# Linear attention and a two-layer squared-ReLU product: Strassen products over pairs of blocks

## The chip, the cores and the metric

The kernel runs on one core of a Trainium2 chip. The metric is the device time of one execution in microseconds (us); of several executions the median counts. Busy times, waits and the order in time come from one profiled execution.

## What is computed

```python
k_s = exp(k - max(k, axis=2)); k_s = k_s / (sum(k_s, axis=2) + 1e-9)      # over the sequence
q_s = exp(q - max(q, axis=-1)); q_s = q_s / (sum(q_s, axis=-1) + 1e-9)    # over the head
kv = einsum('bhsd,bhse->bhde', k_s, v)
x = einsum('bhsd,bhde->bhse', q_s, kv)      # 8 batches, 8 heads, 576 positions, head size 64
x = x.transpose(0, 2, 1, 3).reshape(4608, 512)
out = square(relu(x @ w_in)) @ w_out        # w_in 512 x 2048, w_out 2048 x 512
```

Inputs and output are float32.

## The kernel before

**Blocks.** The 4608 tokens are nine blocks of 512. Block b (0 to 7) holds the first 512 positions of batch b; the 64 positions that each batch leaves over go through a DRAM tensor (`x_left`) and make block 8. In every block the hidden layer has 16 chunks (`fc`) of 128 features. Float32 precision comes from splitting each operand into a rounded part (float32r) and a rest, and adding three products: high by high, high by low, low by high.

**Plain form (blocks 0 and 1).** For a chunk, `h_part` (line 663) makes 4 x 3 products of 512 columns into one PSUM bank; `relu`, `square`, `g_high`, `g_low` (lines 670 to 685) turn the bank into the squares and split them; two steps later `out_part` (line 714) multiplies 4 x 3 times with `wo[fc]` into four accumulator banks (`acc`). One chunk of one block is called a step here; steps are numbered through, 16 to a block.

**Strassen form (blocks 2 to 8).** Two chunks (a beat, `j` = 0 to 7) and two halves of x's 512 input features and two halves of the block's columns make a 2 x 2 by 2 x 2 product, which `strassen` (line 850) does with seven products instead of eight, named A11, S4, S2, A12, S3, S1, A22. Each is 2 x 3 instructions of 256 columns (`product`, line 838). Three banks X, Y, Z (line 848) are shared by all beats: `c1`, `u2`, `u3` copy X, `a12` and `a22` add Z, and `r..`, `m..`, `q..` take ReLU and square. `h0`, `h1` round the squares on ScalarE and `l0`, `l1` make the rests on GpSimd. The sums of w_in that the products need come from `w_sums` (line 761), once, through the DRAM tensor `w_prod`; 14 of the 56 products stay in SBUF, the others are loaded again for every block (`load_products`, `refill`) into four ring tiles. The sums of x (`x_sums`, line 792) are made for every block. w_out (`wo`) stays in SBUF as a whole.

**Attention.** Per batch there are four pairs of heads (`attention`, line 456): loads of k, q, v; maxima and exponentials; a turn of q through DRAM (`bounce_out`, `bounce_in`: one store, four loads); the key product `kv` on TensorE; and four score products, `times` in `parts` (line 594), two of 320 and two of 256 columns, into `x_raw`. It runs one block ahead of its use.

**Order.** All engines execute in program order. Through the string `ORDER` (blocks 0 and a part of 1, up to step 17) `InOrder` chains every instruction behind the one before it on its engine. From there to the end of block 1 a table by step (`AHEAD`, `TWO_AT`, `put`) places attention and sums, unchained; this is the stage of about 144 to 235 us. From block 2 on the string `BLOCK` is run once for each block, chained again. SyncE (SP) issues nearly all DMAs in the same order.

```python
X, Y, Z = (banks[i][:, :HN] for i in (*H_BANKS, Z_BANK))
```

Of the kernel before, what the change touches and what calls it, by code (L numbers as in the profile page):

```python
# [16 lines left out]
P = 128  # L17
# [48 lines left out]
LEFT_AFTER = "x:lB22-"

# [41 lines left out]
BLOCK = """  # L109
A11.0 Lv/2 kr/0 x:hT1- o00.0 c1.0 kp/0 x:lB21- o01.0 kh/0 S4.7- Lk/2 x:hT4- kl/0 S2.0 x:hB22- a12.7- x:lT3- o02.0 w3  # L110
r12.7- u2.0 m12.7- A12.0 l1.7- h0.7- o03.0 r11.0 P0/0 x:lT1- km/1 S3.0 c0/0 o10.0 u3.0 x:lT4- k1/1 S1.0 o11.0 l0.7-
k2/1 A22.0 o12.0 ke/1 r21.0 q21.0 o13.0 a22.0 x:lB22- kx/1 A11.1 m11.0 r22.0 o00.1 q22.0 qd/1 d0/0 c1.1 o01.1 ev0
P1/0 S4.0 h1.0 st0 ev1 c1/0 l1.0 S2.1 a12.0 qx/1 st1 d1/0 o02.1 u2.1 qs/1 P2/0 r12.0 A12.1 XL/0 c2/0 Lq/3 ev2 o03.1
m12.0 qy/1 r11.1 d2/0 S3.1 st2 h0.0 ev3 P3/0 o10.1 u3.1 m11.1 l0.0 st3 c3/0 tb/1 S1.1 o11.1 d3/0 Bw/1 qm/2 A22.1
a22.1 kv/1 r21.1 o12.1 Lv/3 r22.1 kp/1 kr/1 q21.1 o13.1 kh/1 A11.2 q22.1 kl/1 o00.2 c1.2 B/1 h1.1 o01.2 l1.1 S4.1
Lk/3 S2.2 a12.1 qd/2 o02.2 r12.1 w4 u2.2 m12.1 A12.2 qh0/1 km/2 o03.2 Lq/0+ qh1/1 ql0/1 S3.2 k1/2 qx/2 o10.2 w5 h0.1
ql1/1 k2/2 P0/1 u3.2 S1.2 c0/1 o11.2 r11.2 d0/1 l0.1 A22.2 qs/2 P1/1 o12.2 w6 r21.2 c1/1 ke/2 o13.2 q21.2 A11.3
a22.2 qy/2 kx/2 m11.2 o00.3 r22.2 d1/1 c1.3 o01.3 XL/1 q22.2 tb/2 h1.2 P2/1 S4.2 Bw/2 c2/1 l1.2 S2.3 d2/1 w7 a12.2
P3/1 o02.3 u2.3 c3/1 A12.3 r12.2 d3/1 B/2 m12.2 o03.3 r11.3 x:T1 h0.2 S3.3 qm/3 l0.2 o10.3 w8 u3.3 m11.3 S1.3 qd/3
qh0/2 kv/2 w9 a22.3 qh1/2 o11.3 Lv/0+ kr/2 A22.3 r22.3 ql0/2 kh/2 o12.3 o13.3 r21.3 Lq/1+ kl/2 kp/2 qx/3 A11.4 ql1/2  # L120
q21.3 qs/3 o00.4 Lk/0+ q22.3 c1.4 o01.4 h1.3 qy/3 w10 P0/2 S4.3 c0/2 km/3 S2.4 l1.3 o02.4 w11 d0/2 u2.4 A12.4 a12.3
k1/3 r12.3 P1/2 o03.4 r11.4 c1/2 S3.4 m12.3 o10.4 d1/2 h0.3 w12 k2/3 u3.4 S1.4 XL/2 l0.3 P2/2 o11.4 c2/2 tb/3 A22.4
d2/2 Bw/3 o12.4 ke/3 w13 r21.4 q21.4 P3/2 o13.4 a22.4 c3/2 m11.4 kx/3 A11.5 d3/2 r22.4 B/3 o00.5 c1.5 o01.5 q22.4
h1.4 S4.4 l1.4 S2.5 w14 a12.4 qh0/3 o02.5 A12.5 u2.5 ql0/3 r12.4 o03.5 qh1/3 m12.4 w15 kv/3 h0.4 ql1/3 S3.5 Lv/1+
r11.5 kr/3 o10.5 m11.5 kh/3 kp/3 S1.5 l0.4 u3.5 o11.5 a22.5 w16 Lk/1+ kl/3 A22.5 r22.5 q22.5 o12.5 r21.5 qm/0+ q21.5
o13.5 h1.5 A11.6 qd/0+ P0/3 o00.6 w17 c1.6 c0/3 o01.6 l1.5 qx/0+ Lq/2+ d0/3 S4.5 qs/0+ P1/3 S2.6 c1/3 a12.5 qy/0+
o02.6 w18 u2.6 d1/3 r12.5 A12.6 XL/3 m12.5 P2/3 o03.6 h0.5 tb/0+ c2/3 S3.6 l0.5 r11.6 Bw/0+ d2/3 o10.6 m11.6 w19
u3.6 km/0+ P3/3 S1.6 c3/3 o11.6 d3/3 B/0+ A22.6 k1/0+ o12.6 r21.6 k2/0+ q21.6 o13.6 w20 A11.7 a22.6 qh0/0+ o00.7
ke/0+ c1.7 o01.7 x:T2 kx/0+ S4.6 x:T3 r22.6 S2.7 q22.6 w0+ x:T4 h1.6 o02.7 a12.6 u2.7 l1.6 A12.7 qh1/0+ o03.7 r12.6
w1+ ql0/0+ x:hB11 m12.6 S3.7 h0.6 o10.7 u3.7 x:lB11 x:hT2 S1.7 r11.7 o11.7 w2+ x:hB21 a22.7 l0.6 A22.7 m11.7 r22.7  # L130
qm/1+ x:hT3 o12.7 x:lT2 r21.7 o13.7 q21.7 q22.7 kv/0+ ql1/0+ h1.7
# [36 lines left out]
def attention_ffn_kernel(ctx: ExitStack, tc: tile.TileContext, q, k, v, w_in, w_out, out):  # L168
# [25 lines left out]
    NB = 2  # L194
# [261 lines left out]
    def attention(b, pr, two):  # L456
# [130 lines left out]
        def kv_rest():  # L587
            for f in (rs, rr, kf, kv_high, kv_low):
                f()

        def k_pad():
            e.pool.memset(kk[HALF:, :, HIGH, :], -FLT_MAX)

        def parts(g0, nj, h):
# [26 lines left out]

        def keep_left():
            dst = x_left[:, pr, b * LEFT : (b + 1) * LEFT].rearrange("p (g a) -> p g a", g=2)
            e.sp.dma_start(dst, st[0][:, :, LOW])

        quarters = [parts(g0, nj, h) for g0, nj in ((0, LOW), (2, HIGH)) for h in range(2)]

        def attn(m):
            def go():
                for f in quarters[m]:  # L630
                    f()
                if m == 1:
                    keep_left()

            return go
# [475 lines left out]
```

## Time and profile before

| | |
|---|---|
| runs, median (lowest to highest) | 873.58 us (871.17 to 873.65), 3 runs |
| profiled execution, own time | 870.37 us |
| its span, first to last instruction | 868.1 us |
| mean granted TensorE clock | 0.993 |
| TensorE (PE) busy | 847.6 us, 98% |
| VectorE (DVE), ScalarE (ACT), GpSimd (POOL) busy | 512.2, 538.4, 475.4 us |
| DMA | 169.34 MB, mean 195 GB/s |

The profile names engines PE, PEld (weight loads), DVE, ACT, POOL and SP. A row of a stretch table gives busy time and number of instructions by engine in that stretch, the granted clock as a share of 2.4 GHz, the busy share of the DMA engines and what they moved. All instructions stand under one line, since the ordering helper issues them; they are told apart by the names of what they write and read (`bank<-x_T,wp` is a Strassen product, `bank<-wo,g` an output product, `bank<-qs,kvs` a score product).

### The profile page before, as it was taken

To read this page: it belongs to the slowest core of one execution; us is meant where nothing else is said; L and a number is where in the kernel's file an instruction comes from. 1 tells how busy PE (TensorE), PEld (TensorE's weight loads), DVE (VectorE), ACT (ScalarE), POOL (GpSimd) and SP (SyncE) were. 2 spreads that over 40 slices of the span, in tenths; PEclk is the share of its full clock that TensorE was granted. 3 is DMA by queue.
4 is the path that set the end of the run, shared out by engine and by line. 5 is a ranking of instruction groups with operands and counts; after the bars stand their busy time and mean duration, and the time that the engine had idled before them with its cause. 6 is when DMAs were issued, how large, how long until landed. Compare 5 with 4: busy or idle time off the path is not lost.

```text
span 868.1 us, 15842 instructions
## 1 busy us (share of the span) xinstructions
PE 847.6 (98%) x5422; PEld 735.1 (85%) x5422; DVE 512.2 (59%) x1210; ACT 538.4 (62%) x1219; POOL 475.4 (55%) x406
## 2 busy tenths in 40 slices
PE   8999999899699999999999999999999999999997
PEld 6777778788588888888888988888888989989996
DVE  7898889967767557666665666665773221212111
ACT  4888866566566676666666676657666544364442
POOL 4577746897636456744855485448553622262222
PEclk9999999999899999999999999999999999999999
DMA  9979625998758764777478747784666445534551
GB/s 235 269 199 306 185 75 159 291 316 261 249 155 251 240 200 133 234 223 235 117 215 245 238 123 208 244 231 148 175 207 191 132 139 175 178 108 122 170 170 49
DMA packets 128783, 169.34 MB, mean 195 GB/s; under 512 B 50880, under 2 KB 94912, under 8 KB 128576
## 3 DMA queue, kind: packets, MB, share of 16 engines
q1 hardware_dynamic: 127952, 167.39, 65.0%
q10 hardware_dynamic: 752, 0.95, 0.4%
q8 instruction: 43, 0.70, 0.3%
q14 instruction: 36, 0.29, 0.1%
HBM read 135.27 MB, written 33.03 MB: 194 GB/s over the span
## 4 chain that ended last, share of the span: by engine, by line
PE 83%; DVE 5%; DMA 5%; issue 2%; ACT 2%; POOL 2%; SPq 1%; ACTq 0%; POOLq 0%; DVEq 0%
PE bank L148 83%; SPq L148 1%; DMA vt<-in_v_dram 1%; DMA w_prod<-w_sum 1%; DVE w_sum L148 1%; DVE m L148 1%; DMA qT<-bounce 1%; DMA bounce<-tb 1%; DMA qt<-in_q_dram 1%; POOL qn L148 0%; POOL qs L148 0%; DMA wp<-w_prod 0%; DMA w_prod<-wi 0%; DVE qn L148 0%; ACT qn L148 0%
## 5 line engine op out<-in xcount | busy, mean ns | idle before, releaser
L148 PE MATMUL bank<-wo,g 128*128 128x512 f32 x1344 | 366.4, 395 | 0.0
L148 POOL TENSOR_TENSOR g<-c,g 128x512 fp32r<-128x512 f32 x112 | 144.9, 1294 | 259.7 <-ACT g L148 201.4
L148 PEld LDWEIGHTS bank<-wo,g 128*128 128x128 f32 x1344 | 230.7, 189 | 30.1
L148 PEld LDWEIGHTS bank<-x_T,wp 128*128 128x128 f32 x1344 | 186.4, 190 | 23.5 <-ACT bank L148 9.3
L148 PE MATMUL bank<-x_T,wp 128*128 128x256 f32 x1344 | 197.5, 283 | 8.6 <-ACT bank L148 8.6
L148 PEld LDWEIGHTS bank<-x_B,wp 128*128 128x128 f32 x1008 | 141.8, 190 | 15.0 <-ACT c L148 2.3
L148 PE MATMUL bank<-x_B,wp 128*128 128x256 f32 x1008 | 148.5, 283 | 0.8 <-ACT c L148 0.7
L148 DVE TENSOR_TENSOR c<-c,bank 128x256 f32<-128x256 f32 x168 | 67.6, 415 | 109.2 <-PE bank L148 58.4
L148 ACT ACTIVATE c<-bank 128x256 f32<-128x256 f32 x168 | 64.7, 385 | 90.5 <-PE bank L148 75.2
L148 POOL TENSOR_TENSOR qs<-qT,qs 64x640 fp32r<-64x640 f32 x48 | 77.2, 1609 | 21.2 <-ACT qs L148 13.4
L148 DVE TENSOR_TENSOR bank<-bank,c 128x256 f32<-128x256 f32 x56 | 23.9, 426 | 108.0 <-PE bank L148 108.0
L148 PE MATMUL bank<-x_hi,wi 128*128 128x512 f32 x256 | 87.5, 399 | 0.0
L148 PE MATMUL bank<-wo,g_hi 128*128 128x512 f32 x256 | 81.6, 402 | 0.0
L148 ACT ACTIVATE c<-c 128x256 f32<-128x256 f32 x168 | 66.7, 414 | 14.7 <-DVE c L148 12.4
L148 ACT COPY c<-bank 128x256 f32<-128x256 f32 x112 | 41.6, 371 | 53.9 <-PE bank L148 53.4
L148 ACT CAST g<-c 128x512 fp32r<-128x512 f32 x112 | 69.3, 619 | 8.5 <-DVE c L148 7.1
L148 DVE TENSOR_TENSOR x_raw<-bank,xf 64x256 f32<-64x256 f32 x96 | 39.6, 412 | 34.1 <-ACT xf L148 31.0
L148 PEld LDWEIGHTS bank<-x_hi,wi 128*128 128x128 f32 x256 | 48.4, 189 | 10.8 <-DVE x_lo L148 0.4
L148 PEld LDWEIGHTS bank<-wo,g_hi 128*128 128x128 f32 x256 | 47.8, 192 | 10.4 <-ACT g_hi L148 0.4
L148 POOL TENSOR_TENSOR qn<-qn,qs 128x640 f32<-128x640 f32 x30 | 40.2, 1340 | 24.9 <-DVE qs L148 12.2
L148 ACT COPY xf<-bank 64x320 f32<-64x320 f32 (+1 forms) x96 | 38.0, 396 | 23.9 <-PE bank L148 22.0
L148 ACT CAST qs<-qT 64x640 fp32r<-64x640 f32 x48 | 34.8, 726 | 28.3 <-DMA qT<-bounce 27.7
(123 smaller groups left out, 1206.9 us busy)
## 6 DMA issues: line engine op xcount, KB each, us to landing
wp<-w_prod SPq DMA_DIRECT2D x155, 512.0 KB, 4.2
out_dram<-o SPq DMA_DIRECT2D x68, 128.0 KB, 2.4
raw_i<-in_moe_w_in_dram SPq DMA_DIRECT2D x16, 512.0 KB, 6.5
raw_o<-in_moe_w_out_dram SPq DMA_DIRECT2D x16, 512.0 KB, 6.5
w_prod<-w_sum SPq DMA_DIRECT2D x32, 256.0 KB, 2.9
bounce<-tb SPq DMA_DIRECT2D x24, 320.0 KB, 3.4
qT<-bounce SPq DMA_DIRECT2D x96, 80.0 KB, 2.2
w_prod<-wi SPq DMA_DIRECT2D x24, 256.0 KB, 3.3
```

The lines of the kernel that those rows point to most:

```text
L148: ins = f(*args, **kwargs)
```

## The change

- Blocks 0, 1 and 2 are in plain form; blocks 3 to 8 are three pairs of neighbouring blocks in Strassen form. The two column halves are now the two blocks of a pair, 512 columns each (`FIRST_WIDE`, `wide`, `x_units`).
- A beat gives both blocks' squares. Those of the first block go into the output products at once; those of the second wait in SBUF (`far`), are split later (`hf`, `lf`), and their 16 x 12 output products follow when the pair's eight beats are done.
- The rests `l..` and `lf..` of the squares are made on VectorE; in plain steps from 18 on ReLU and square work in the PSUM bank, both on ScalarE.
- w_out is written to DRAM once (`keep`), five chunks of it at four places aside (`KEPT` stays, `BACK` comes back into block 1's x tiles), and streamed with the w_in products through seven ring tiles, 46 loads of 512 KB for each pair (`refill`).
- x of blocks 3 to 7 goes through DRAM (`XR`, `bring`). Blocks 3 and 4 make their scores with three full products (`three`) instead of two half-filled ones; the others as before.
- One string (`LIST`) states the order of everything from step 18 to the end, chained on all engines. `w_sums` is cut into single units that `LIST` spreads over steps 18 to 42.

```diff
-HN = 256
 NPR = 8
-PRODUCTS = ("A11", "S2", "A12", "S3", "S1", "A22", "S4")
...
+NB = 2
+PRODUCTS = ("A11", "S4", "S2", "A12", "S3", "S1", "A22")
...
+KEPT = 5, 10, 14
+BACK = 1, 3, 8, 12
+RING = "o9", "o11", "i14", "o12", "i15", "o13", "o15"
+FIRST_WIDE = 3
+THREE = 3, 4
...
+PAIR = "A11 S4 o1 S2 A12 o1 S3 S1 o1 o1 A22 o0 o0 o0 o0".split()
+TAIL = "S4 o1".split()
...
+LIST = """
+P0/2.0 qm/2.2 w0.a2 w0.WA h18_0 c0/2.0 h18_1 d0/2.0 qd/2.2 km/2.2 P1/2.0 h18_2 c1/2.0 h18_3 d1/2.0 w0.s1 Lq/3.0
...
+        def three(g0, nj):
+            def times():
+                ps = st[g0] = next_bank("a")[:, : 2 * nj * BLK]
+                for i, (kl, ql) in enumerate(((0, 0), (0, 1), (1, 0))):
+                    qs = st["q"][ql][:, g0 : g0 + 2, :nj].rearrange("p g j a -> p g (j a)")
+                    out = ps.rearrange("p (g f) -> p g f", g=2)
+                    e.pe.matmul(out, kvs[:, kl], qs, start=(i == 0), stop=(i == 2))
...
     def square(s):
...
-            e.act.activation(s["r"], s["r"], AF.Square)
+        if s["n"] >= BEGIN:
+            s["r"] = s["ps"]
+            e.act.activation(s["ps"], s["ps"], AF.Square)
             return
...
+    def refill(s, n):
+        kind, i = tiles_of[n]
+        tag = RING[(s * len(tiles_of) + n) % len(RING)]
+        t = stay.tile([P, 2, 2, 2 * P], F32R, name="wp", tag=tag)
+        if kind == "w":
+            e.sp.dma_start(t.bitcast(F32), w_prod[i])
+            for k in range(2):
+                held[s, used[2 * i + k]] = t[:, k]
+        else:
+            e.sp.dma_start(t.rearrange("p a b f -> p a (b f)").bitcast(F32), w_outs[i % NFC])
+            wo_at[s, i] = t.rearrange("p a b f -> p a (b f)")
...
+    X, Y, Z = (banks[i] for i in (X_BANK, Y_BANK, Z_BANK))
...
             c1=lambda: e.act.copy(Y, X),
-            u2=lambda: e.act.copy(c(0)[:, 1], X),
-            u3=lambda: e.act.copy(c(1)[:, 1], X),
...
+            u2=lambda: e.act.copy(far(0), X),
+            u3=lambda: e.act.copy(far(1), X),
+            r11=act(n_(0), at(Y), AF.Relu), m11=tt(n_(0), n_(0), at(Y), ALU.mult),
+            r21=act(n_(1), at(X), AF.Relu), m21=tt(n_(1), n_(1), at(X), ALU.mult),
+            a22=tt(f_(1), f_(1), at(Z), ALU.add), a12=tt(f_(0), f_(0), at(Z), ALU.add),
...
+    for token in LIST:
+        run(token)
```

By count, TensorE's instructions of 512 columns on x and w_in go from 384 to 1584, those of 256 columns from 2352 to none; the 1728 output products stay; score products go from 96 to 112.

**TensorE inside a beat.** First the kernel before, in the second half of the program: from S4 over S2, A12, S3, S1 to A22, with output products in groups of three (bank_90 is X, bank_92 Y, bank_96 Z).

```order
L148 MATMUL bank_96<-x_B_2558,wp 128x256 x6
L148 MATMUL bank_90<-x_T_2553,wp 128x256 x6
L148 MATMUL bank_93<-wo_866,g 128x512 x3
L148 MATMUL bank_92<-x_B_2554,wp 128x256 x6
L148 MATMUL bank_94<-wo_866,g 128x512 x3
L148 MATMUL bank_90<-x_T_2555,wp 128x256 x6
L148 MATMUL bank_91<-wo_1082,g 128x512 x3
L148 MATMUL bank_96<-x_T_2556,wp 128x256 x6
```

Now the changed kernel, from an output group behind S4 over S2 and A12 to the next output group; each product is six instructions of 512 columns.

```order
L294 MATMUL bank_91<-wo_955,g 128x512 x3
L294 MATMUL bank_90<-xh_T_3766,wp 128x512
L294 MATMUL bank_90<-xl_T_3837,wp 128x512
L294 MATMUL bank_90<-xh_T_3766,wp 128x512 x2
L294 MATMUL bank_90<-xl_T_3837,wp 128x512
L294 MATMUL bank_90<-xh_T_3766,wp 128x512
L294 MATMUL bank_92<-xh_B_3301,wp 128x512
L294 MATMUL bank_92<-xl_B_3202,wp 128x512
L294 MATMUL bank_92<-xh_B_3301,wp 128x512 x2
L294 MATMUL bank_92<-xl_B_3202,wp 128x512
L294 MATMUL bank_92<-xh_B_3301,wp 128x512
L294 MATMUL bank_95<-wo_955,g 128x512 x3
```

Before, S2 follows S4 at once and an output group parts it from A12; now an output group stands between S4 and S2, and A12 follows S2 at once.

**VectorE beside attention.** Before, in a block with attention: the additions and multiplications of the beat are 256 wide (`c`, `bank_96`), between the score additions (`x_raw`, `xf`) and the attention's own work.

```order
L148 TENSOR_TENSOR c_5228<-c_5228,bank_92 128x256
L148 TENSOR_TENSOR x_raw<-bank_89,xf 64x2x4x32
L148 TENSOR_TENSOR xf<-bank_89,xf 64x2x32
L148 STREAM_TRANSPOSE tb<-qn 128x5x4x32
L148 TENSOR_TENSOR x_raw<-bank_89,xf 64x2x4x32
L148 TENSOR_TENSOR bank_96<-bank_96,c_5228 128x256
L148 TENSOR_TENSOR x_raw<-bank_89,xf 64x2x4x32
L148 TENSOR_TENSOR c_5228<-c_5228,bank_96 128x256
```

Now the first pair of blocks: `c<-c,bank_92` is `m11`, `g<-c,g` is `l0`, `far` is `a22`, and `c<-c,bank_90` is `m21`, which reads X and stands ahead of the next A11.

```order
L294 TENSOR_TENSOR c<-c,bank_92 128x512
L294 TENSOR_TENSOR xr<-bank_89,xf 64x2x4x32
L294 TENSOR_TENSOR g<-c,g 128x512
L294 TENSOR_REDUCE m_4791<-m_4739 32x4 x4
L294 TENSOR_REDUCE mt<-m_4791 128x128
L294 STREAM_TRANSPOSE mb<-mt 128x128
L294 TENSOR_TENSOR far<-far,bank_96 128x512
L294 TENSOR_TENSOR xr<-bank_89,xf 64x2x4x32
L294 STREAM_TRANSPOSE tb<-qn 128x5x4x32
L294 TENSOR_TENSOR c<-c,bank_90 128x512
```

The rests of the squares have come to VectorE's list, the second multiplication as well, and the next A11 of TensorE waits for the latter.

## Rows read from the trace of the kernel before

**Rows 1.** The page, its head and part 1 (engine, busy us, share, instructions).

```profile
span 868.1 us, 15842 instructions
...
PE 847.6 (98%) x5422; PEld 735.1 (85%) x5422; DVE 512.2 (59%) x1210; ACT 538.4 (62%) x1219; POOL 475.4 (55%) x406
```

**Rows 2.** Table of stretches: length, busy us by engine, PEclk, DMA share, GB/s.

```profile
50.00:150.00 100.00, 99.91 (x509) 80.41 (x508) 87.82 (x161) 76.41 (x146) 66.20 (x54) 1.00 0.63 181
150.00:200.00 50.00, 47.83 (x256) 38.83 (x255) 39.79 (x80) 32.01 (x65) 44.10 (x40) 0.97 0.92 290
300.00:350.00 50.00, 50.00 (x346) 44.77 (x345) 32.02 (x84) 33.03 (x81) 29.99 (x26) 1.00 0.60 174
700.00:750.00 50.00, 50.00 (x313) 45.05 (x312) 8.98 (x21) 21.56 (x54) 12.92 (x10) 1.00 0.48 153
```

**Rows 3.** TensorE in order of time: start us, us, instruction; two steps' first products.

```profile
115.37 0.39 PE L148 MATMUL bank<-x_hi,wi 128*128 128x512 f32 x1
...
120.81 0.39 PE L148 MATMUL bank<-x_hi,wi 128*128 128x512 f32 x1
```

**Rows 4.** TensorE in order of time: S4 of two beats that follow each other.

```profile
718.63 0.88 PE L148 MATMUL bank<-x_B,wp 128*128 128x256 f32 x6
719.34 0.88 PE L148 MATMUL bank<-x_T,wp 128*128 128x256 f32 x6
...
729.18 0.88 PE L148 MATMUL bank<-x_B,wp 128*128 128x256 f32 x6
```

**Rows 5.** TensorE in order of time, 156 to 238 us: waits in square brackets.

```profile
156.59 0.80 PE L148 MATMUL bank<-vt,ke 128*64 128x65 f32 x20
...
165.70 0.38 PE L148 MATMUL bank<-qs,kvs 128*128 128x320 f32 x1 [1.49 <-ACT kvs L148]
166.77 0.51 PE L148 MATMUL bank<-qs,kvs 128*128 128x320 f32 x1 [0.69 <-DVE kvs L148]
...
170.63 0.62 PE L148 MATMUL bank<-wo,g_hi 128*128 128x512 f32 x2
...
234.82 1.65 PE L148 MATMUL bank<-x_T,wp 128*128 128x256 f32 x6 [8.32 <-ACT bank L148]
...
237.54 1.05 PE L148 MATMUL bank<-wo,g_hi 128*128 128x512 f32 x2
```

**Rows 6.** TensorE in order of time: two score products and what follows each.

```profile
261.38 0.31 PE L148 MATMUL bank<-qs,kvs 128*128 128x320 f32 x1
261.53 0.87 PE L148 MATMUL bank<-x_T,wp 128*128 128x256 f32 x6
...
267.25 0.28 PE L148 MATMUL bank<-qs,kvs 128*128 128x256 f32 x1
267.37 0.88 PE L148 MATMUL bank<-x_B,wp 128*128 128x256 f32 x6
```

**Rows 7.** TensorE and ScalarE in order of time: A22's end and its ReLU.

```profile
736.24 1.55 PE L148 MATMUL bank<-wo,g 128*128 128x512 f32 x6
736.44 0.39 ACT L148 ACTIVATE c<-bank 128x256 f32<-128x256 f32 x1 [2.44 <-PE bank L148]
```

**Rows 8.** Groups by line and form: busy us, mean ns | idle before.

```profile
L148 ACT COPY o<-bank 128x512 f32<-128x512 f32 x18 | 10.5, 586 | 9.7 <-PE bank L148 5.8 <-DMA bounce<-tb 2.9 <-DMA out_dram<-o 0.8
L148 DVE TENSOR_TENSOR r<-r,bank 128x512 f32<-128x512 f32 x16 | 10.9, 679 | 0.4 <-ACT r L148 0.4
L148 DVE TENSOR_TENSOR w_sum<-a,w_sum 128x512 fp32r<-128x512 f32 x8 | 9.4, 1180 | 3.6 <-ACT w_sum L148 3.5
L148 POOL TENSOR_TENSOR g<-c,g 128x512 fp32r<-128x512 f32 x112 | 144.9, 1294 | 259.7 <-ACT g L148 201.4 <-issue 42.9 <-PE bank L148 11.8
```

**Rows 9.** The page's part 6: DMA issues, size, median us to landing.

```profile
wp<-w_prod SPq DMA_DIRECT2D x155, 512.0 KB, 4.2
```

**Rows 10.** SyncE's queue by tile: ns of one issue, shortest/median/longest, first and last start.

```profile
L148 SPq DMA_DIRECT2D vt<-in_v_dram x120: 533/606/1651, 10.5 to 618.9; - x120
L148 SPq DMA_DIRECT2D qT<-bounce x96: 302/422/633, 129.3 to 655.0; - x96
```

**Rows 11.** VectorE by tile `T`: ns of one, shortest/median/longest, first and last start.

```profile
L148 DVE TENSOR_TENSOR T<-x_raw,T x14: 679/683/1741, 231.1 to 757.7; 128x512 f32<-128x512 f32 x14
```

More of the change, by code (lines that the diff above doesn't have):

```diff
@@ L115 @@
[L115 to L119, printed above, removed]
@@ L561, in kf, with kv_clear @@
             e.dve.tensor_scalar_mul(st["kf"], st["kv"][:, :D], st["rs"])
+        def kv_clear():
+            z = kvs.bitcast(F32)
+            if b in THREE:
+                e.pool.memset(z[HALF:, :, :D], 0.0)
+                e.pool.memset(z[:HALF, :, D:], 0.0)
+            else:
+                e.pool.memset(z[HALF:, 0, D:], 0.0)
+                e.pool.memset(z[:HALF, 1, D:], 0.0)
         def kv_high():
+            if b in THREE:
+                for h in range(2):
+                    e.act.copy(kvs[half[h], 0, half[h]], st["kf"][half[h]])
+                return
             for h in range(2):
@@ L622, in keep_left, with x_part @@
+        def x_part(t, g0):
+            return spread_out(t[0][:, pr])[:, g0 : g0 + 2]
         def keep_left():
             dst = x_left[:, pr, b * LEFT : (b + 1) * LEFT].rearrange("p (g a) -> p g a", g=2)
[L624 to L635, printed above, removed]
@@ new lines, in attention_ffn_kernel, with keep_out @@
+    order += [("o", fc + NFC) for fc in range(NFC)]
+    tiles_of = []
+    for kind, n in order:
+        if (kind, n) not in tiles_of and (kind == "w" or n % NFC not in KEPT + BACK):
+            tiles_of.append((kind, n))
+    w_prod = dram.tile([len(used) // 2, P, 2, 2, 2 * P], F32, name="w_prod")
+    w_outs = dram.tile([NFC, P, 2, NT], F32, name="w_outs")
+    w_at = {u: i for i, u in enumerate(used)}
+    held, wo_at, back = {}, {}, {}
+    def keep_out(fc):
+        e.sp.dma_start(w_outs[fc], wo[fc].bitcast(F32))
@@ L998, in attention_ffn_kernel @@
-    put(2 * 2 * NFC - 5, keep)
-    put(2 * 2 * NFC - 2, keep_last)
-    for n in range(NFC + LAG, 2 * NFC):
-        gs[n] = ffn_h(*steps[n])
-        m = n - LAG
-        for u in slots.get(2 * n, []):
-            u()
-        ffn_out(*steps[m], gs.pop(m))
-        for u in slots.get(2 * n + 1, []):
-            u()
-    ring = (len(USED) - KEPT) // 2
-    def refill(blk, n):
-        if blk <= B:
-            at = (blk - 2) * ring + n
-            load_products(KEPT + 2 * n, 2, f"i{RING[at % len(RING)]}", stay)
@@ L1073, in attention_ffn_kernel @@
-    for x in e.all:
-        x.last, x.chained = None, True
-    for blk in range(2, B + 2):
-        for token in BLOCK:
-            if blk <= B or token[-1] == "-" or token[0] == "o" or token[:2] in ("ev", "st"):
-                run(blk, token)
-            if blk == B - 1 and token == LEFT_AFTER:
-                load_left()
+    for fc in KEPT:
+        wo_at[fc] = wo[fc]
+    pairs = {(2, pr): third[pr][1] for pr in range(NB)}
+    for b in range(2, B):
+        for pr in range(NPAIR):
+            if (b, pr) not in pairs:
+                pairs[b, pr] = attention(b, pr, True)[1]
```

786 lines of the change are left out of this document (474 added, 312 removed).

## Prediction

> **What bounds the kernel now.** The page comes first: TensorE is busy 98% of an 868.1 us span [rows 1]. The second view is the stretch table, since a share is a mean over stages [rows 2]. Between 50 and 150 us TensorE is busy 99.9 of 100 us although the vector engine (DVE) is busy 87.8 of the same 100; at 300 to 350 us it is busy 50.00 of 50. The row of 150 to 200 us shows a loss. So in nearly all of the span a saving has to come out of TensorE's own instructions, and in one stage out of waits.
>
> The third view is TensorE in order of time. In the plain stage one step is 24 products of 512 columns and takes 120.81 - 115.37 = 5.44 us, 0.2267 each [rows 3]. In the Strassen stage one beat is 42 products of 256 columns and 24 of 512, from one pair of x_B groups to the next: 729.18 - 718.63 = 10.55 us [rows 4]. At the clock level of 2.4 GHz (granted 1.00 in rows 2) the columns alone would take 42 x 0.1067 + 24 x 0.2133 = 9.60 us; the rest, 0.95 us over 66 instructions, is 0.0144 us for each. The plain step gives 0.2267 - 0.2133 = 0.0134. I read this as a fixed cost of 0.0134 to 0.0144 us for each product, whatever its width.
>
> The waits: one score product waits 1.49 us and the next 0.69 us, and the first Strassen group waits 8.32 us [rows 5]. Behind each the products run at half pace for a while. From 166.77 to 170.63 there are one score product and nine wide ones, 0.15 + 9 x 0.227 = 2.2 us, but they took 3.86. From 234.82 to 237.54 twelve 256-wide ones, 2 x 0.71 = 1.42 by rows 4, took 2.72. Waits of 10.5 us cost 10.5 + 1.7 + 1.3 = **13.5 us** in all.
>
> **The change part by part.** *Columns.* In the last six blocks two beats (84 narrow and 48 wide products, 21.10 us) become one of 90 wide ones. At 0.2267 to 0.2277 each that is 20.40 to 20.49; I take 20.45, as no row shows 512-wide Strassen groups. There are 8 x 3 = 24 such beats: 24 x 0.65 = **-15.6 us**. The third block (index 2) loses its Strassen form: 8 x 10.55 = 84.4 us become 384 x 0.2272 = 87.2: **+2.8**. Blocks 3 and 4 use three full score products where there were two half ones. The former cost 261.53 - 261.38 = 0.15 and 267.37 - 267.25 = 0.12 each [rows 6]; eight pairs get one more of each: 8 x 0.27 = **+2.2**. Together -10.6 us, bounds -12 to -9 from the two per-product figures.
>
> TensorE's fixed cost is where a page speaks against the change. The Trainium skill ("TensorE: Matmul & The Clock Gate", section "Back-to-back issue gap") gives an isolated gap of the columns plus 2.5 ns. An estimate from that page has a beat of 9.77 us and would leave this part of the sum at about +4 us instead of -10.6. Rows 4 show 10.55, so the trace does not agree here, and the measured beat decides.
>
> *Eviction of the 512-wide beats.* All products of a beat go through the same three banks as before, and each copy is now 512 wide. S2 may not write X until `c1` has copied it; the cover is S4 and one output group, 6 x 0.227 + 3 x 0.227 = 2.04 us. ScalarE starts 736.44 - 736.24 = 0.20 us after the last issue of a group [rows 7], and a 512-wide copy from a bank takes 0.586 us [rows 8]: 0.8 us. The same holds for `u2` before S3. `r21` and `m21` (0.586 for a pass of ScalarE and 0.679, rows 8) must be through before the next A11: 0.2 + 0.6 + 0.7 and two handovers, 1.6 us, under four output groups of 2.72 us. I cost these at nothing. What is left over is 1.1 to 1.2 us, so an engine that is late by more than that shows in TensorE. In pairs 2 and 3 of blocks nothing competes; in the first the attention does.
>
> *Load of the other engines.* The squares' low parts move from GpSimd (112 x 1.29 us, rows 8) to DVE. DVE's load for one pair of heads comes from two stretches: 32.02 us of 50 with attention and 8.98 without [rows 2], so 23 us more in 50; a block is 8 x 10.55 = 84.4 us, which makes 39 us for its four pairs of heads, 9.7 each, x sums included. From step 18 to the first wide product TensorE has 30 h steps and 31 outputs, 732 products and the attention's, about 186 us. DVE has some 12 pairs x 9.7 = 116, 30 low parts at 0.68 = 20, for the sums of w_in 16 instructions at up to 1.18 [rows 8], 19 at most, and 16 for x at 0.68, 11: 166 us, or 89%. SP issues eight input transfers for each pair of heads at 0.61 and four returns at 0.42 [rows 10], with the rest some 8 us, 12 x 8 = 96; with some 100 shorter ones for w_prod, w_out and the stores about 150 of 186 us. In the first wide pair DVE is near 80 to 85% again; after it, without attention, under a third. The streamed w_out and products are 46 loads of 512 KB in 168 us, 0.14 MB/us; they wait in seven ring tiles, some 20 us ahead of use, so I cost them at nothing. Without that cover a load of 4.2 us [rows 9] would stand in front of TensorE each time.
>
> *Waits.* The table-driven stage from 144 to 235 us disappears, and with it the place of the 13.5 us: sums of w_in and x that were made in 83 us now have 186, and between the last sum for S2 and S2 itself stand 14 output and h groups and A11, some 10 us of TensorE's work. New waits are bounded by two rows. Below: the fully ordered stretch 50 to 150 us lost 0.1 of 100 with DVE at 88%. Above: 150 to 240 lost 13.5 with DVE at 80% in the row of 150 to 200. Over the 360 us until attention ends that is 0.4 to 54 us. I take **+5**, close to the lower row, because the order there is written out on all engines, as it is in the changed stage.
>
> **Sum:** -15.6 + 2.8 + 2.2 - 13.5 + 5 = -19.1. The profiled execution took 870.37 us: 851.3. The median of the runs shown, 873.58, stands 3.2 above it; with that, **854 us**.
>
> **Rivals.** *(a) DVE falls behind.* DVE work on 512 columns has a median of 683 ns and a longest of 1741 [rows 11]. Some 140 instructions with two SBUF operands stand in the 360 us. If a quarter meet a GpSimd instruction, at 1.06 us each, DVE gets 37 us more on top of about 310, 347 of 360, which leaves nothing for its own waits. Squares' low parts then come late: 8 to 15 us of waits instead of 5, and the clock's return with them, 861 to 870. For it speaks the DVE share; against it, 50 to 150 us. The Trainium skill ("SBUF — State Buffer", section "SBUF: two separate sides") says that the loser of the port shared by DVE and GpSimd blocks for the whole instruction; the longest of rows 11, 1.06 us above the median, would fit a wait behind most of one GpSimd instruction of 1.29 (rows 8).
>
> *(b) Width saves nothing.* If the 0.95 us of a beat is not per instruction but something that 512 columns keep, only columns count: (3312 - 2112 - 1176) x 0.2267 = +5.4, +2.2 for the scores, -13.5 and +5: 869.5, as a median 873, no change. Against it: the plain step has the same remainder per product.
>
> *(c) Slower: score products wait for their keys.* In the old stage the key product of a pair of heads came at 156.59 and its two score products at 165.70 and 166.77, after waits of 1.49 and 0.69 us and with 1.7 us of slow products behind them [rows 5]: 3.9 us. In the new order a pair has about 6 us between them, and about 20 pairs stand in stages where DVE is at 80 to 90%. If eight of them are as late, it is 31 us instead of 5: 880. It decides from seven on. Against it: the ordered stretch has pairs of heads too, and no wait.
>
> **How the numbers follow.** The forecast has 0.66, (a) 0.16, (b) 0.07, (c) 0.11. The range 845 to 871 goes from the sum with no new wait and the lower column figure (849, less 3 to 4 for a run as short as the profiled one) to the end of (a); it leaves out (b) and (c), 0.18. A measurement of this kernel tells 0.3%, 2.6 us, from no change. Faster takes the forecast, all but 0.01 of (a) and 0.02 of (b): 0.83; same is the rest of both, 0.06; slower is (c), 0.11.
>
> **What would show it.** Right: 90 products of a wide beat in 20.4 to 20.5 us in the last two pairs of blocks, no wait near 235 us, TensorE's granted clock at 1.00 behind 160 us, a last product near 843 us. Wrong: (a) TensorE waiting for `g_lo` or `c` of DVE between 144 and 510 us; (b) a beat of 21 us; (c) waits for `kvs` in front of `qs,kvs`. A ring load that lands late in the last pairs would contradict the cover of the stream.

## The result, and the profile after

The changed kernel takes **865.71 us** (median of 7 runs, 863.45 to 868.47), the kernel before 873.54 in the same comparison (7 runs): ratio **0.9917 (0.9892 to 0.9943)**. (In brackets stands a 95% interval; the ratio is formed from all runs and so differs a little from that of the two medians.) Forecast were 854 us and 19 us of gain; measured are 8. Its profiled execution took 863.45 us, where the sum of the prediction gave 851.3.

The page's head and first part, after (before: [rows 1]):

```profile
span 861.7 us, 13013 instructions
PE 838.3 (97%) x4286; PEld 677.9 (79%) x4286; DVE 552.3 (64%) x1155; ACT 491.9 (57%) x932; POOL 288.0 (33%) x275
```

TensorE's busy share fell from 98 to 97%, though it has 9.3 us less to do by this count: part of what was saved is idle now. The stretch table (columns as in [rows 2]) says where:

```profile
50.00:150.00 100.00, 98.10 (x515) 78.44 (x515) 87.93 (x161) 76.21 (x146) 62.45 (x51) 1.00 0.66 184
150.00:200.00 50.00, 48.41 (x271) 38.82 (x267) 39.34 (x101) 33.78 (x71) 34.39 (x37) 1.00 0.85 260
200.00:250.00 50.00, 47.94 (x267) 38.59 (x263) 39.11 (x100) 27.53 (x58) 32.87 (x34) 1.00 0.81 240
250.00:300.00 50.00, 44.10 (x262) 34.66 (x260) 37.77 (x91) 28.30 (x61) 28.50 (x28) 1.00 0.85 246
300.00:350.00 50.00, 49.05 (x230) 39.47 (x231) 42.72 (x95) 30.21 (x58) 25.54 (x26) 1.00 0.88 270
350.00:500.00 150.00, 150.00 (x780) 122.51 (x779) 120.72 (x283) 102.58 (x196) 47.38 (x39) 1.00 0.89 266
500.00:550.00 50.00, 47.72 (x258) 38.06 (x258) 37.94 (x82) 27.21 (x55) 15.81 (x13) 1.00 0.66 194
700.00:750.00 50.00, 50.00 (x222) 41.42 (x221) 14.47 (x21) 22.62 (x38) 0.00 (x0) 1.00 0.56 177
```

From 350 to 500 us and behind 550 TensorE never stops. It loses from 140 to 350, the largest part from 250 to 300 (5.9 of 50 us), and 2.3 us near 515. The vector engine is not busier there than in 50 to 150 (88%): from 150 to 300 it is below 80%, from 300 to 350 at 85%.

The wide beats are as forecast. TensorE in order of time, each row the twelve output products that end the beat's 66 products, those of the first block and of the Strassen part:

```profile
716.31 2.88 PE L294 MATMUL bank<-wp,g 128*128 128x512 f32 x12
731.27 2.88 PE L294 MATMUL bank<-wp,g 128*128 128x512 f32 x12
```

14.96 us for 66 products are 0.2267 each; with the second block's 24 the beat takes 20.40 where 20.45 was forecast and two old ones took 21.10 [rows 4]. The view of waits shows none of TensorE's behind 530 us, so no eviction and no ring tile made it wait in the last pairs.

TensorE's waits from 125 to 530 us (us in total, times, longest), where [rows 5] had 10.5 in three:

```profile
PE bank L294 <- DVE kvs L294: 6.2, 7, 1.7
PE bank L294 <- ACT kvs L294: 4.4, 3, 1.8
PE bank L294 <- ACT kt L294: 2.4, 1, 2.4
PE bank L294 <- DMA vt<-in_v_dram: 0.7, 2, 0.5
PE bank L294 <- DVE xf L294: 0.6, 1, 0.6
PE bank L294 <- DVE g_lo L294: 0.2, 1, 0.2
```

14.5 us. The last output products begin at 853.67 us, so TensorE ends near 856.4, 13.4 behind the forecast of 843. The 24 beats gave 24 x 0.05 = 1.2 us more than forecast. If the terms for the third block and the score products are as forecast, new losses are 5 + 13.4 + 1.2, some **19.6 us** instead of 5: the 14.5 of the view and some 5 of slower products behind waits and short gaps, which were not taken apart.

One wait, followed back through the changed kernel's timeline (start in us, length in us, engine, line, operation; in brackets at the end of a row the idle time ahead of it in us and what ended it). SyncE's issues:

```profile
285.43 1.75 SPq L294 DMA_DIRECT2D bounce<-tb  x1
287.23 0.53 SPq L294 DMA_DIRECT2D w_outs<-wo  x1
287.84 1.51 SPq L294 DMA_DIRECT2D qt<-in_q_dram  x2
289.46 1.99 SPq L294 DMA_DIRECT2D qT<-bounce  x4
291.49 0.43 SPq L294 DMA_DIRECT2D xl_T<-x_raw  x1
292.02 1.25 SPq L294 DMA_DIRECT2D kt<-in_k_dram  x2
```

The vector engine in the same stretch:

```profile
297.50 1.26 DVE L294 TENSOR_REDUCE m<-kt 128x128 f32<-128x640 f32 x1 [3.01 <-DMA kt<-in_k_dram]
299.06 0.28 DVE L294 TENSOR_SCALAR kf<-bank,rs 128x64 f32<-128x64 f32 x1
```

ScalarE:

```profile
299.38 0.51 ACT L294 CAST kvs<-kf 64x64 fp32r<-64x64 f32 x2 [3.71 <-DVE kf L294]
```

TensorE:

```profile
299.94 0.56 PE L294 MATMUL bank<-qs,kvs 128*128 128x320 f32 x2 [1.73 <-ACT kvs L294]
```

SyncE issues one transfer behind the other with gaps of 0.04 to 0.11 us. The key load of a later pair of heads goes out at 292.02 and lands about 297.4. The vector engine, which follows its one order, stands for it at the key maximum, 3.01 us, and behind that instruction stand `rs` and `kf` of the pair whose score product is next; ScalarE's `kvs` and TensorE then wait in turn. In the vector engine's waits from 125 to 350 us this form leads:

```profile
DVE m L294 <- DMA kt<-in_k_dram: 15.6, 6, 3.7
DVE g_lo L294 <- ACT g_hi L294: 7.2, 12, 1.3
DVE qm L294 <- DMA qt<-in_q_dram: 3.8, 1, 3.8
```

### The profile page after: what moved, and what is told of

The parts are those of the page before. It is cut to its first block, busy times and chain, and to the rows that moved or that the text cites. A ratio compares the mean times of both kernels' runs of the same rounds, so it can differ in the third digit from the quotient of the medians.

```text
span 861.7 us, 13013 instructions
## 1 busy us (share of the span) xinstructions
PE 838.3 (97%) x4286; PEld 677.9 (79%) x4286; DVE 552.3 (64%) x1155; ACT 491.9 (57%) x932; POOL 288.0 (33%) x275
## 4 chain that ended last, share of the span: by engine, by line
PE 73%; DVE 10%; DMA 6%; SPq 4%; issue 3%; ACT 2%; POOL 1%; DVEq 0%; POOLq 0%; ACTq 0%
PE bank L294 73%; SPq L294 4%; DVE m L294 2%; DMA qt<-in_q_dram 1%; DMA raw_o<-in_moe_w_out_dram 1%; DMA kt<-in_k_dram 1%; DVE g_lo L294 1%; DMA xl_B<-x_raw 1%; DVE qm L294 1%; POOL qn L294 1%; DMA vt<-in_v_dram 1%; ACT bank L294 1%; DMA raw_i<-in_moe_w_in_dram 1%; DVE w L294 1%; DVE qs L294 1%
## 5 line engine op out<-in xcount | busy, mean ns | idle before, releaser
L294 PE MATMUL bank<-wp,g 128*128 128x512 f32 x648 | 160.8, 390 | 0.0
L294 PEld LDWEIGHTS bank<-wp,g 128*128 128x128 f32 x648 | 120.8, 188 | 25.3
L294 PE MATMUL bank<-xh_T,wp 128*128 128x512 f32 x384 | 131.5, 392 | 0.0
L294 POOL TENSOR_TENSOR qs<-qT,qs 64x640 fp32r<-64x640 f32 (+1 forms) x40 | 64.2, 1604 | 107.8 <-ACT qs L294 88.3
L294 PE MATMUL bank<-xh_B,wp 128*128 128x512 f32 x288 | 97.9, 390 | 0.0
L294 PEld LDWEIGHTS bank<-xh_T,wp 128*128 128x128 f32 x384 | 72.1, 188 | 16.2 <-ACT bank L294 1.0
L294 PEld LDWEIGHTS bank<-wo,g_hi 128*128 128x128 f32 x384 | 69.8, 188 | 14.5 <-ACT g_hi L294 0.4
L294 PE MATMUL bank<-wo,g_lo 128*128 128x512 f32 x192 | 75.3, 392 | 0.0
L294 PE MATMUL bank<-x_lo,wi 128*128 128x512 f32 x192 | 75.0, 391 | 0.0
L294 PE MATMUL bank<-xl_T,wp 128*128 128x512 f32 x192 | 74.8, 390 | 0.0
L294 PE MATMUL bank<-wo_back,g 128*128 128x512 f32 x288 | 72.0, 391 | 0.0
```

The costliest lines, as they stand in the source:

```text
L294: ins = f(*args, **kwargs)
```

## The experiments

All are edits of the changed kernel and were timed beside the kernel before, whose median was 873.7 to 875.1 us. "Against the change" is the difference of the two ratios times 873.5 us; each ratio has an interval of some 2 us either way, so a difference under some 3 us is not clear of noise.

| run | us | ratio to before | against the change |
|---|---|---|---|
| the change | 865.71 | 0.9917 (0.9892 to 0.9943) | |
| e1_keys_early | 865.33 | 0.9902 (0.9877 to 0.9926) | -1.3 |
| e2_max_later | 868.15 | 0.9932 (0.9909 to 0.9955) | +1.3 |
| e3_keys_later | 878.43 | 1.0053 (1.003 to 1.0076) | +11.9 |
| e4_less_vector | 870.33 | 0.9959 (0.9942 to 0.9976) | +3.7 |
| e5_halves | 877.51 | 1.0032 (1.0014 to 1.005) | +10.0 |
| e6_products_later | 869.94 | 0.9941 (0.992 to 0.9962) | +2.1 |
| e7_short_max | 863.34 | 0.9864 (0.9842 to 0.9887) | -4.6 |
| e8_later_and_early | 870.73 | 0.9952 (0.9934 to 0.9969) | +3.1 |
| e9_later_mended | 865.13 | 0.9894 (0.9872 to 0.9915) | -2.0 |
| e10_later_and_loads | 865.44 | 0.9894 (0.9877 to 0.991) | -2.0 |
| e11_maxima_unused | 866.0 | 0.9893 (0.9866 to 0.992) | -2.1 |
| e12_act_stores | 863.78 | 0.9882 (0.986 to 0.9903) | -3.1 |
| e13_act_own | 862.61 | 0.9871 (0.9849 to 0.9893) | -4.0 |
| e15_more_issues | 901.64 | 1.0309 (1.0274 to 1.0343) | +34.2 |
| e16_act_own_later | 862.87 | 0.988 (0.9857 to 0.9902) | -3.2 |
| e17_fewer_issues | 856.88 | 0.9809 (0.9786 to 0.9831) | -9.4 |
| e19_act_own_x | 861.57 | 0.9859 (0.9834 to 0.9884) | -5.1 |

**The width.** e5_halves: each 512-wide product of the Strassen part becomes two.

```diff
-                e.pe.matmul(
-                    ps, w[:, a, f], x[:, cc], start=start and cc == 0 and k == 0,
+                for c in (slice(0, NT // 2), slice(NT // 2, NT)):
+                    e.pe.matmul(
+                        ps[:, c], w[:, a, f], x[:, cc, c], start=start and cc == 0 and k == 0,
```

> The changed kernel with each of the 1008 products of 512 columns that make h in the last six blocks split into two of 256 columns on the same bank; order, copies and output products unchanged. Theory width (a product costs its columns and a fixed part): 1008 more products; by 0.1183 us for a 256-wide one (twice that less 0.2267 is 0.0099) or 0.1217 (0.0167), 10 to 17 us longer, 876 to 883 us, a beat of 20.8 to 21.1 us in the last pair where it is 20.40. Theory columns (rival b of the prediction): 864 to 868 us and a beat of 20.4.

Measured: 877.51 us. Both halves open their sum on one bank, which changes the sums and not the work. The beat in the last pair:

```profile
729.21 2.91 PE L294 MATMUL bank<-wp,g 128*128 128x512 f32 x12
744.78 2.91 PE L294 MATMUL bank<-wp,g 128*128 128x512 f32 x12
```

15.57 us where 14.96 stood: 0.61 for 42 more products, 0.0145 each, at the same columns. That is near what the prediction read from [rows 3, 4] (0.0134 to 0.0144), and rival (b) falls: width does save. A little of the 0.61 is not in the split products, since twelve output products take 2.91 us here and 2.88 in the changed kernel.

**Key loads earlier, the key maximum later, key loads later.** The first theory from the chain above: loads are issued too short ahead. In the order's tokens (`Lk` key load, `km` key maximum, `kp` padding, `kv` key product):

```diff
 e1: the load of pair 3.2, whose buffer kv/3.0 frees
-kv/3.0 w1.h12 h27_3 qx/3.2 kr/3.0 ... kp/3.0 h28_2 w1.l34 Lk/3.2 h28_3 kl/3.0
+kv/3.0 w1.h12 h27_3 kp/3.0 Lk/3.2 qx/3.2 kr/3.0
 e2: its maximum
-qh0/3.1 km/3.2 h29_0 ... kv/3.1 k1/3.2
+kv/3.1 km/3.2 k1/3.2
 e3: its load
-Lk/3.2 h28_3 kl/3.0 ... ke/3.1 Bw/3.2 c0/3.0 o.26.2 XL/3.0
+ke/3.1 Bw/3.2 c0/3.0 o.26.2 Lk/3.2 XL/3.0
```

> The changed kernel with each key load (and the padding memset ahead of it) moved up in the stated order to just behind the key product that frees its buffer; the lead from load to key maximum grows from some 4 us of TensorE's work to some 9. Theory A (key loads are issued too short ahead, the vector engine stands at the key maximum, and the score products' keys stand behind it in its order): the vector engine's waits for kt between 125 and 350 us fall from 15.6 to under 4 us, TensorE's waits there from about 12.5 to 5 to 8, time 855 to 860 us. Theory B (the vector engine simply has too much work): its waits for kt go, but the keys stay late, 864 to 867 us.

> The changed kernel with each key maximum moved down on the vector engine to just ahead of the next step of its chain; loads as they are, the lead grows by 1 to 5 us, 2.5 on average. Theory A: about half to two thirds of the vector engine's 15.6 us of waits for kt go, 858 to 863 us. Theory B: 864 to 867 us, the vector engine's work is the same.

> The changed kernel with each key load 2.5 to 3 us of TensorE's work later in the stated order (never behind its use). Theory A: some 15 of 20 pairs of heads hold the vector engine 3 us longer, its waits for kt grow from 15.6 to over 45 us between 125 and 350, TensorE's waits by 15 to 35, 880 to 900 us. Theory B: 864 to 870 us.

Measured: e1 865.33, e2 868.15, e3 878.43 us. In e1 the vector engine's waits for kt fell to

```profile
DVE m L290 <- DMA kt<-in_k_dram: 1.8, 1, 1.8
```

and TensorE's waits from 125 to 530 us did not fall, 14.8 us instead of 14.5:

```profile
PE bank L290 <- DVE kvs L290: 5.1, 5, 1.7
PE bank L290 <- ACT kvs L290: 3.2, 2, 1.8
PE bank L290 <- ACT kt L290: 3.1, 1, 3.1
PE bank L290 <- DMA vt<-in_v_dram: 1.6, 2, 1.1
```

The time moved by less than the intervals. Behind the early key loads the other transfers went out later: TensorE's waits for vt doubled, and the vector engine's for qt grew from 3.8 to 5.9 us. e2 had less of the wait for kt (10.0) and the same time. e3 shows that a late key load does cost (waits for kt 28.6 us from 125 to 350, and 878.43 us, between the two ranges expected). So late key loads are one link, but theory A, that they are the cause, falls.

**Less work on the vector engine.** e4_less_vector drops ten small reductions of each key maximum; e7_short_max keeps every instruction and shortens two:

```diff
 e7
-            e.dve.tensor_reduce(m, kk.rearrange("p h j d -> p h d j"), axis=AX.X, op=ALU.max)
+            e.dve.tensor_reduce(m, kk[:, :, :1].rearrange("p h j d -> p h d j"), axis=AX.X, op=ALU.max)
-            e.dve.tensor_reduce(qm, qq, axis=AX.X, op=ALU.max)
+            e.dve.tensor_reduce(qm, qq[:, :, :, :8], axis=AX.X, op=ALU.max)
```

> The changed kernel without ten of the small reductions of the key maximum in every pair of heads from the third block on (the keys' exponentials then take another offset): 1.8 us less work on the vector engine for each pair, some 20 of its 9.7, loads and order unchanged. Theory A: the vector engine comes to the key maximum earlier and waits there longer for the same load; its waits for kt grow from 15.6 us, time 861 to 866 us. Theory B: the waits of TensorE fall to a few us, 853 to 858 us.

> The changed kernel with the key maximum taken over one fifth of the keys and the query maximum over an eighth of the head's width, from the third block of heads on: the same instructions in the same order, 1.7 us less work on the vector engine for each pair of heads, some 24 us of its 184 between 125 and 350. The exponentials then take another offset. Theory B: TensorE's waits from 125 to 530 us fall from 15 to under 6, 853 to 859 us. Theory A or C: they fall by at most a third, 861 to 866 us. The same rate of TensorE as in the changed kernel (0.2267 us for a product) is expected by all.

Measured: e4 870.33, slower, for another reason (last section). e7 863.34: with the vector engine at 104.43 us of 145 to 300 where the changed kernel had 120.94, TensorE's waits fell only from 14.5 to 12.6:

```profile
PE bank L294 <- DVE kvs L294: 7.2, 7, 1.7
PE bank L294 <- ACT kt L294: 3.1, 1, 3.1
```

and its waits for kt rose to 23.3 us: it comes earlier and waits longer. Theory B expected 853 to 859. The vector engine's load has a share, some 2 to 5 us, and is not the main cause. The changed kernel itself says the same: from 350 to 500 us the vector engine is at 80%, as from 150 to 300, and TensorE loses nothing.

**Score products later.** The third theory: each product stands a little too early in TensorE's order. In the tokens, `P0` is the first score product of a pair of heads, `c0` the copy behind it, and `Lv` the load of values.

```diff
 e9, two of eleven places
-tb/5.0 P0/4.3 k1/5.0 relu41 Bw/5.0 o.39.0 w7.s1 rm41 o.39.1 w7.s2 c0/4.3 k2/5.0 o.39.2
+tb/5.0 k1/5.0 relu41 Bw/5.0 o.39.0 w7.s1 rm41 o.39.1 w7.s2 k2/5.0 o.39.2 P0/4.3
-kv/4.1 w5.s4 ... w5.h12 Lv/4.3 kp/4.1 o.35.3
+w5.s4 ... w5.h12 o.35.3 kv/4.1 Lv/4.3 kr/4.1
```

> The changed kernel with the first score product of nine pairs of heads (all of the first four blocks of heads that waited) put 0.4 to 6 us of TensorE's work later, just ahead of its pair's second, and two key products that waited 1.3 and 2.6 us later; the other engines keep their work, a few copies move behind them. Theory C (each wait is its own product that stands some 0.5 to 2.5 us too early in TensorE's order, whatever made its keys late): TensorE's waits between 125 and 350 us fall from 12.3 to under 5 us and the slow products behind them go too, 856 to 860 us. Theory B (the vector engine has too much work, so lateness is handed on): the waits come back at other products, 863 to 867 us.

> Both edits: score products later as in the run before, key loads early as in the first experiment. Theory C: as the products alone or 1 to 3 us better, 854 to 859 us, since a late load then has two covers. Theory B: 863 to 867 us.

> As the run e6_products_later, without its two new waits: there the key product of one pair stood behind the load of the values that takes its buffer (11.2 us, and that pair was computed with the wrong values), and the last copies of the first pair came too late. Here nine first score products stand 0.7 to 2 us later, the first pair's first three together 1.4 to 2, the two key products 0.7 and 2.7 us, with the loads behind them, and two low parts of x on GpSimd, which ran beside the keys of a pair near 515 us, 4 us later. Theory C: TensorE's waits from 125 to 530 us fall from 16 to under 6, 854 to 859 us. Theory B: 863 to 867 us.

> The edit of e9_later_mended, and the key loads of the stretch from some 225 us on early as in e1_keys_early. Theory C: within 2 us of e9_later_mended, 853 to 859 us, as most of the waits that the loads cause have gone already.

Measured: e6 869.94, e8 870.73; both had a key product behind a load of values, as the third text says, which cost one wait of 11.2 us in e6 and of 9.5 in e8. e9 865.13 and e10 865.44. Of the old waits in e9 most have gone, and others have come, 13.7 us in all:

```profile
PE bank L290 <- DVE g_lo L290: 3.8, 2, 2.8
PE bank L290 <- DVE xf L290: 3.4, 3, 1.9
PE bank L290 <- ACT kt L290: 3.1, 1, 3.1
PE bank L290 <- DVE kvs L290: 2.9, 4, 1.1
```

Lateness is handed on. Theory C falls too, and the next theory is that something which all these places share is late.

**SyncE's queue.** What they share is the queue that issues their transfers. Summing the times of SyncE's single issues gives its share of a stretch (a timeline row that holds several issues also holds the gaps between them, so the rows' lengths give more). In the changed kernel it is 0.41 from 100 to 145 us, then 0.89 (145 to 200), 0.87 (200 to 250), 0.84 (250 to 300), 0.66 (300 to 345) and 0.56 from 350 to 500, where TensorE loses nothing. In the kernel before it is 0.40, 0.84, 0.44, 0.56 and 0.41 up to 345 us. The edits:

```diff
 e12 and e13 (own blocks of w_in); e12 also the stores of sums, some 1.3 us later
-                e.sp.dma_start(w_prod[pair, :, place], t.bitcast(F32))
+                e.act.dma_start(w_prod[pair, :, place], t.bitcast(F32))
 e15 (more issues, same bytes)
-                e.sp.dma_start(qT[c * BLK : (c + 1) * BLK].rearrange("p g j a -> p g (j a)"), src)
+                for g in (slice(0, 2), slice(2, 4)):
+                    e.sp.dma_start(dst[:, g], src[:, g])
 e17 (fewer issues)
-            for c in range(4):
+            for c in range(4 if b == 2 else 2):
```

> The changed kernel with the 88 stores of w_prod issued by ScalarE instead of SyncE, the 64 of sums some 1.3 us of TensorE's work later so that ScalarE need not wait for them. By the trace they take 24 issues at 0.65 and 64 at 0.43 us, 43 us of SyncE's queue between 140 and 300. Theory D (the queue of SyncE is full and everything it issues is late): SyncE's share there falls from 0.88 to 0.94 to some 0.65, TensorE's waits from 125 to 530 us from 16 to under 8, 854 to 860 us, unless ScalarE (57 percent busy before, some 80 with the issues) makes relu and g_hi late. Theories B and C: 864 to 868 us.

> Of these only the 24 stores of w_in's own blocks (16 us of the queue, nearly all between 140 and 195 us) are issued by ScalarE, at their old places. Theory D: the waits near 157 and 174 us go (1.6 us and some slow products), those behind 225 us stay, 861 to 865 us. Theories B and C: 864 to 868 us.

> The changed kernel with each returned quarter of qT brought by two transfers of half the size: four more issues for each pair of heads, some 1.8 us of SyncE's queue each, the same bytes. Theory D: between 145 and 300 us eleven pairs need 20 us more of a queue that has 10 to 18 left, so waits grow by 8 to 25 us, 873 to 890 us. Theories B and C: 864 to 869 us.

> The changed kernel with two of the four returned quarters of qT left out from the fourth batch on (half of the query rows of those score products are then stale): two issues of some 0.45 us less for each of 20 pairs of heads, nothing put on another engine, all else as it is. Theory D (the queue of SyncE sets the lateness): from 190 to 300 us some 8 us of the queue come free of 110, waits of TensorE there fall from 12 to about 6, 857 to 862 us. Theories B and C: 864 to 867 us.

Measured: e15 **901.64**, e17 **856.88**, e13 862.61, e12 863.78 us. In e15 the eight returns of q for one pair of heads take 3.84 us of the queue, where four took 1.99 above:

```profile
259.39 3.84 SPq L294 DMA_DIRECT2D qT<-bounce  x8
```

96 more issues at a median of 0.42 are 40 us of queue, and the time grew by 34, to above the 890 expected. TensorE's waits grew from 14.5 to 34.5 us, within the growth of 8 to 25 expected; with them the granted clock fell, to 0.93 from 250 to 300 us, where the changed kernel has 1.00. The waits stand at every kind of place:

```profile
PE bank L294 <- DVE kvs L294: 10.9, 10, 2.4
PE bank L294 <- ACT kvs L294: 5.3, 4, 2.6
PE bank L294 <- DVE xf L294: 4.2, 4, 1.3
```

The bytes are the same, and the DMA engines' share from 145 to 300 us was lower (0.75 instead of 0.84), so it is the issuing and not the moving. The changed kernel's key loads agree. From issue to landing they take, from 50 to 145 us and then from 145 to 300:

```profile
DMA to landing us min/median/max: 2.6/2.9/5.2
DMA to landing us min/median/max: 2.8/3.1/5.0
```

Once issued, a key load is not slower in the stretch that loses. e17 leaves two of four returned quarters of q out from the fourth batch on, so half of those query rows are stale: 40 issues less, 17 us of queue at the same median, and nothing is put elsewhere. 9.4 us come back, and TensorE's waits fall to 9.9, led by

```profile
PE bank L294 <- DVE kvs L294: 5.0, 6, 1.7
PE bank L294 <- ACT kvs L294: 2.3, 2, 1.8
```

e15 and e17 also change the return of q itself, for which the score products wait. e13 and e12 leave it alone and move issues and no byte. With 24 of them on ScalarE the queue's share from 145 to 200 falls to 0.64 and the wait near 174 us goes (the one near 157, also expected to go, stays); the time falls by 4.0 us. With 88 the share is 0.58 to 0.66 up to 300 us and the vector engine waits only 4.0 us for kt, but e12 misses the 854 to 860 expected, since now ScalarE is late, for which the vector engine waited 7.2 us before:

```profile
DVE g_lo L291 <- ACT g_hi L291: 17.5, 15, 3.4
```

The Trainium skill ("Perfetto Trace Analysis", section "DMA Optimizations") says that spreading transfers over the engines that can issue them may help where generating descriptors is the limit. e13 agrees with that by its 4.0 us, and e12 shows the price. The same section of the Trainium skill says that splitting transfers may let some start sooner, and ties an earlier end to DMA engines that are generally idle. Here they were at 0.84 and the issuing queue had little room, and splitting 96 transfers (e15) cost 34 us.

**A version that beats both kernels.** e16 adds to e13 those moves of e9 that had brought no new wait; e19 adds instead 16 stores whose source ScalarE has copied itself:

```diff
-            e.sp.dma_start(dst, src)
+            (e.act if b in THREE else e.sp).dma_start(dst, src)
-            e.sp.dma_start(x_raw[b][pr // 2][:, pr % 2], st["xr"])
+            (e.act if b in THREE else e.sp).dma_start(x_raw[b][pr // 2][:, pr % 2], st["xr"])
```

> The edit of e13_act_own (24 stores issued by ScalarE), and from e9_later_mended the moves that had brought no new wait: five first score products 1 to 2 us later, two key products with the loads behind them, and the two low parts of x on GpSimd near 515 us. Theory D with local leads on top: 857 to 862 us, below both e13 and e9. If the lateness is only handed on: 862 to 866 us.

> The edit of e13_act_own, and the 16 stores of x and of its last columns for the fourth and fifth batch, which ScalarE has itself copied out of PSUM, are issued by ScalarE as well, at their old places in the order: some 0.4 us each, 7 us of SyncE's queue between 190 and 300 us on top of the 16 before 195. Theory D: as e17 in that stretch, which took 8 us off the queue, 857 to 861 us; a part may be given back by ScalarE, which has the issues now. Not D: 862 to 866 us.

Measured: e16 862.87, no better than e13 alone. e19 **861.57** us, ratio 0.9859 (0.9834 to 0.9884): its interval lies below that of the change. It is just over the 857 to 861 expected; TensorE's waits are 10.6 us, with 149.26 us busy of 145 to 300 where the change had 145.45. So the queue is shown to be a cause by moving issues alone, with 5.1 us. That it makes all of the new losses is not shown: e17, the largest gain, leaves 9.9 us of waits.

## Why the prediction was half right

- **Columns: the sum right, the mechanism only in part.** A beat takes 20.40 us against 20.45 forecast, and halving the products again costs 0.0145 each. But one fixed cost for every product is not what the kernel before shows. Six narrow products take 0.71 us there (719.34 less 718.63 in [rows 4]), 0.118 each, and six output products 1.39, 0.232 each:

```profile
725.69 1.55 PE L148 MATMUL bank<-wo,g 128*128 128x512 f32 x6
727.08 0.88 PE L148 MATMUL bank<-x_B,wp 128*128 128x256 f32 x6
```

In the changed kernel's beats a 512-wide product takes 0.2267. So of the 0.70 us saved in a beat some 0.42 came from the width (84 x 0.1183 less 42 x 0.2267), 10 us of the program, and some 0.28 from 48 output products that kept their width and ran faster, nearly 7 us. The prediction's mean over 66 instructions held both by luck. Why the output products ran faster was not tested.

- **Eviction and ring: right.** No wait for `c`, and none for a ring tile, in the last two pairs.
- **The old waits: right.** The wait of 8.32 us and the two before it [rows 5] have gone with their stage. What stands near 140 to 175 us now is new.
- **New waits, "+5, close to the lower row": wrong, and this is the step that failed.** It measured about 19.6. The row chosen as nearest, 50 to 150 us [rows 2], was chosen by the vector engine's share and by its being ordered. The vector engine was forecast at 89% of the new stage and was at 78% from 140 to 330 us, so a fuller vector engine than forecast did not make the waits. By SyncE's share the row is far off: 0.68 in 50 to 100 and 0.40 in 100 to 145, against 0.84 to 0.89 in the new stage up to 300 us. The prediction had that load right ("about 150 of 186 us" is 0.81, from [rows 10]; over 145 to 345 it measured 0.82) and gave it no price. The step should have asked what stands behind a late transfer in an order that binds every engine. The price depends on which issues change: a microsecond of queue added cost some 0.85 us (e15: 34 for 40), one taken off gave some 0.55 (e17: 9.4 for 17), and issues moved to ScalarE gave less (e19: 5.1 for 40 issues). The 9.4 us of e17 are about half of the 19.6; for the other half no run shows the cause.
- **Rival (a), the vector engine falls behind:** its time, 861 to 870, is the one measured, but not its mechanism; 16.5 us less work there from 145 to 300 us gave 2 to 5 us (e7). Vector instructions stretched beside GpSimd are seen at one wait of TensorE, 1.73 us near 515 us: there the two that make the low parts of `kvs` take 2.52 us beside GpSimd work and elsewhere, from 289.12 us, 0.43. In e9 they take 2.57 beside other GpSimd work, and TensorE, which reaches that product later, does not wait.
- **Rival (c), score products wait for their keys:** the place is right, 13 of the 14.5 us stand in front of score and key products. Its price was too high, and its cause, a lead that is too short, was not it: longer leads (e9) moved the waits and changed the time by 2.0 us, which is not clear of noise.
- **Left open:** the wait near 140 us, where ScalarE copies an output tile that waits for a buffer; how the 5 us outside the view of waits divide; what makes the 9.9 us of waits that e17 leaves; and whether the queue can be emptied without another engine paying. GpSimd as an issuer was not tried.

## What to carry to other kernels

Before pricing an ordered stage, sum the issue time of the queue that feeds it as if it were an engine. Here, at 0.84 to 0.89 of its time, its transfers came late, and in one stated order a late one stops an engine that others wait for; at 0.56 nothing was lost. When waits move from place to place under reordering and the time does not, look for the resource that the places share. Moving issues to another engine gains only as far as that engine stays in time itself: 24 and 40 issues on ScalarE gained, 88 gained no more.

## What the runs showed of the hardware

e4_less_vector, with ten small vector instructions of each pair of heads left out, ran TensorE slower through the whole program. Its output groups near the end, in TensorE's timeline:

```profile
839.09 2.95 PE L294 MATMUL bank<-wo_back,g 128*128 128x512 f32 x12
841.88 2.95 PE L294 MATMUL bank<-wp,g 128*128 128x512 f32 x12
```

Those of the changed kernel:

```profile
837.35 2.88 PE L294 MATMUL bank<-wp,g 128*128 128x512 f32 x12
840.07 2.88 PE L294 MATMUL bank<-wo,g 128*128 128x512 f32 x12
```

2.79 us for twelve products against 2.72, both at a granted clock of 1.00, and from 50 to 125 us, ahead of the edit, a median of 0.232 for a product against 0.227. Its seven runs lie at 868.5 to 872.3 us although TensorE waited only 8.5 us. One run asked whether the numbers or the program did it:

```diff
-            e.dve.tensor_reduce(mt, m5.broadcast_to([P, 4, BLK, 1]), axis=AX.X, op=ALU.max)
             e.dve.transpose(mb.rearrange("p h o (e a) -> p (h o e) a", a=BLK), mt)
+            e.dve.tensor_reduce(mt, m5.broadcast_to([P, 4, BLK, 1]), axis=AX.X, op=ALU.max)
```

> The run e4_less_vector with its ten reductions put back but their result not used: the numbers are those of that run, the instructions those of the changed kernel (two of them change places). It asks why TensorE took 0.2308 us for a product in that run, before its edit begins too, and 0.2267 in all the others. If the numbers make the difference: 0.2308 again and 870 to 878 us. If the program does: 0.2267 and 864 to 868 us.

Measured: 866.0 us and 0.2267 us for a product again, with the numbers of e4. So it came with the instructions, not with the data; by what way was not settled. The kernel before runs its output products in Strassen beats at the same rate, 0.232; whether that is the same effect is not known. A run that leaves instructions out can differ in more than their cost: e7, which shortened them instead, kept the rate.
